# One PSUM pool, copied-out values, additions in thirds and one ranking tile per half in a fused attention and routed feed-forward kernel

## The chip, the cores and the metric

The kernel runs on one core of a Trainium2 chip. The metric is the device time of one execution in microseconds (us); of three runs before the change the median is 877.36 us (875.94 to 880.07). All times below are us unless ns is written. Engines: PE is TensorE (PEld its weight loads), DVE is VectorE, ACT is ScalarE, POOL is GpSimd, SP is SyncE, which issues most of the DMAs.

## The reference, cut to what matters

```
B, H, S, D = 8, 8, 1152, 64;  Sp = 576;  Dm = 512;  F = 1024;  capacity = 128
q_pool = q.reshape(B, H, Sp, 2, D).mean(axis=3)
attn   = softmax(q_pool @ k.T / sqrt(D))              # 576 x 1152 for each head
x      = attn @ v                                     # joined over heads: (B, 576, 512)
for b in range(B):
    scores  = x[b] @ w_gate
    top     = the 128 rows of largest score
    out[b]  = x[b]
    out[b, top] += sigmoid(scores[top]) * (relu(x[b, top] @ w1) @ w2)
```

All is float32.

## The kernel before

**Pairs and halves.** The class `_Plain` does the work (a second path, `_any_scores`, is entered only if the softmax sums leave a safe range). Two heads are a pair: the eight images `b` have four pairs each, and a pair is done in two halves of 288 pooled query rows, so there are 64 halves, 8 in each image. `run()` writes the order out by hand, and each engine executes its own list in that order. One turn `h` of its loop does `scores(h)`, `folded(h)`, then `weighted(h-1)`, `drained(h-1)` and `between(...)`. On PE this gives the score matmuls of one half, the value matmuls of the half before it, then whatever `between` adds.

**Scores (L724 to L740).** Nine tiles, each of two banks of PSUM for the two heads. PE fills a tile (`sc<-qT,kT`), ACT takes the exponent into `p`. The pool `ps_sc` has three such tiles, so the matmuls of the fourth wait for the exponents of the first, and so on.

**Sums (`folded`, L755 to L781).** POOL adds the tiles 0 to 2 to the tiles 3 to 5 of `p` in one instruction (`acc`, 128x1728), DVE folds the tiles 6 to 8 (`fold<-p`) and `acc` (`fold<-acc`), and makes `sum`.

**Values (`weighted`, L742 to L753; `drained`, L783 to L791).** 36 matmuls accumulate `av` in the one tile of the pool `ps_av`; DVE transposes it from PSUM into `avb`.

**A finished pair (`normalized`, L793 to L834).** After each second half PE makes the row sums (`ps<-sum,merge`, L796) in the one tile of the pool `ps_ms`, DVE copies them (`sums`) and inverts them (`rec`), POOL makes `x` and then `prod` (L828), DVE reduces that to `part` (L834). Behind it DVE's list goes on with what `between` adds, then with the transposes `kT` and `qT` of the next pair (`prepare_pair`, every second half), whose `qp` POOL adds after `prod`. The score matmuls of the next pair need `qT`.

**Routing (`routed`, L844 to L1033).** It is a generator, started when an image's last pair is finished. `between`, called once in each half, sends each generator in `self.routing` one piece further. The pieces before the change are, in the eight halves after the start:

1. L870: the score row, spread by PE, copied by ACT to `sc_row`.
2. L656: five small transposes into the tile `ps` (the one of L796), copied by DVE to `gate_sc`; the gate's exponent on ACT (L887); ranking tiles 0 and 1 on DVE. A ranking tile is two comparisons `cmp` and a `tie`, which reads `sc_row` and `before` from SBUF.
3. Ranking tiles 2 and 3.
4. Ranking tile 4, `meta`, and the selection matrices `pick`.
5. L953: ten small matmuls make the list `index` and `own_gate`; POOL gathers the chosen rows `xe` by DMA (L965).
6. L980: `xe` transposed by PE, copied by ACT to `xeT`.
7. L992: first feed-forward layer, 64 matmuls in one two-bank tile, with two ACT instructions (L1000).
8. L1007: second layer, 16 matmuls; DVE adds it to `xe` (L1014), POOL scatters it (L1022).

After the loop `ending` is set and the rest of the routing runs without pauses between ranking tiles.

Of the kernel before, what the change touches and what calls it, by code (L numbers as in the profile page):

```python
# [10 lines left out]
P = 128  # L11
BLK = 32

G = 3
F32 = mybir.dt.float32
# [519 lines left out]
class _Plain:  # L535
# [10 lines left out]
    def __init__(self, ctx, tc, q, k, v, moe_w_gate, moe_w1, moe_w2, capacity, out):  # L546
# [54 lines left out]
    def constants(self):  # L601
# [29 lines left out]
        self.columns(self.token, line_f, self.misc())  # L631
# [92 lines left out]
    def scores(self, half):  # L724
# [4 lines left out]
        for c in range(self.NC):  # L729
            sc = self.ps_sc.tile([P, 2, 512], F32, name="sc")  # L730
# [11 lines left out]
    def weighted(self, half):  # L742

        nc, n = self.nc, self.HALF
        half["av"] = self.ps_av.tile([P, 512], F32, name="av")
        for c in range(self.NC):
            for j in range(2):
                nc.tensor.matmul(  # L748
                    half["av"][j * self.D : (j + 1) * self.D, 0:n],
# [4 lines left out]
                )  # L754

    def folded(self, half):
# [3 lines left out]
        acc = self.work.tile([P, G * 2 * self.HALF], F32, name="acc")  # L760
        groups = p.rearrange("p g u j n -> p g (u j n)")
# [4 lines left out]
        for a, of in enumerate((groups[:, 2, :], acc[:, :])):  # L766
            nc.vector.tensor_reduce(  # L767
                fold[:, a, :],
                of.rearrange("p (m d) -> p m d", d=BLK),
                AX.X,  # L770
                ALU.add,
                apply_transpose=True,
            )
# [9 lines left out]
    def drained(self, half):  # L783
        pair, n, hb = half["pair"], self.HALF, self.HB
        if half["s"] == 0:
# [3 lines left out]
            half["av"][:, 0:n],  # L789
# [48 lines left out]
    def misc(self):  # L838
        return self.ps_ms.tile([P, 512], F32, name="ps")

    def wide(self):
        return self.ps_sc.tile([P, 2, 512], F32, name="sc")

    def routed(self, b, xs, part):  # L844
# [23 lines left out]
        ps = self.wide()  # L868
# [18 lines left out]
        nc.scalar.activation(gate[:, :], gate[:, :], AF.Exp, scale=-1.0)  # L887
# [4 lines left out]
        for t, rows in tiles:  # L892
# [32 lines left out]
            if t % 2 == 1 and not self.ending:  # L925
                yield
        nc.vector.tensor_scalar(
# [11 lines left out]
        for s0, w in self.slots:  # L939

            pick = ffn.tile([P, NT, P], F32, name="pick")
            for t, rows in tiles:
# [6 lines left out]
                )  # L949
            at_ps = yield  # L950
# [27 lines left out]
            pv = self.wide()[:, 0, :].rearrange("p (c n) -> p c n", n=P)  # L978
# [8 lines left out]
            for f0 in range(0, self.NFC, 8):  # L987
                pv = self.wide().rearrange("p b (c n) -> p (b c) n", n=P)
                nf = min(8, self.NFC - f0)
                for f in range(nf):  # L990
# [8 lines left out]
                    if f % 4 == 3:  # L999
                        nc.scalar.activation(  # L1000
# [181 lines left out]
```

## Time and profile before

| | us |
|---|---|
| three runs, median | 877.36 |
| three runs, range | 875.94 to 880.07 |
| profiled execution, its own time | 876.72 |
| profiled execution, span of its instructions | 874.90 |
| PE busy in the span | 786.5 |
| DVE busy | 504.4 |
| POOL busy | 396.1 |
| ACT busy | 345.0 |

The span is what the trace shows; 1.82 us of the profiled execution lie around it. The views read are the busy table of the page, the busy time by stretch, the chain of waits and the timelines of single engines. In a timeline row the first two numbers are the start, in us from the span's start, and the duration; the bracket is the idle time of the engine just before, and what ended it.

### The profile page before, as it was taken

The numbers are of one execution on the slowest core, as the hardware profiler recorded it, in microseconds if no ns is written. First come the engines' busy times: TensorE is split into PE (matmuls) and PEld (weight loads), VectorE is DVE, ScalarE is ACT, GpSimd is POOL, SyncE is SP. The second block draws the span as 40 slices with busy tenths as digits, with TensorE's granted clock in tenths as the row PEclk, the third lists the DMA queues.
The fourth block names the chain that finished last, engine by engine and source line by source line (L and its number), as shares of the span: only waits on it lengthen the run. The fifth ranks groups of instructions, "written<-read, shape, count | busy, mean of one in ns | idle before, by whom it ended". The sixth has DMA issues, their size and how long they took to land.

```text
span 874.9 us, 13669 instructions
## 1 busy us (share of the span) xinstructions
PE 786.5 (90%) x5503; PEld 478.2 (55%) x5503; DVE 504.4 (58%) x848; ACT 345.0 (39%) x617; POOL 396.1 (45%) x188
## 2 busy tenths in 40 slices
PE   6979979899798998899988999889979899799936
PEld 4545545565455654565555655556545565456634
DVE  3556666735677347762667535774556836576250
ACT  5435445342444243442443334443345342445000
POOL 3546645444555254552444535453535445554110
PEclk9999999999999998999998999899999999999968
DMA  9997786674767578395764928849286773761020
GB/s 135 255 144 106 102 146 92 98 96 101 98 72 115 75 132 97 51 129 63 148 95 54 121 42 148 96 76 124 56 123 88 102 96 93 102 77 26 14 79 16
DMA packets 453545, 84.95 MB, mean 97 GB/s; under 512 B 450656, under 2 KB 450656, under 8 KB 453216
## 3 DMA queue, kind: packets, MB, share of 16 engines
q1 hardware_dynamic: 447456, 79.20, 62.6%
q0 software_dynamic: 1280, 4.20, 1.7%
q10 hardware_dynamic: 4736, 0.59, 0.7%
q8 instruction: 45, 0.74, 0.4%
q14 instruction: 28, 0.23, 0.1%
HBM read 72.42 MB, written 20.97 MB: 107 GB/s over the span
## 4 chain that ended last, share of the span: by engine, by line
PE 58%; DVE 14%; POOL 11%; ACT 7%; DMA 4%; issue 3%; SPq 2%; ACTq 0%; POOLq 0%; DVEq 0%
PE sc L733 24%; PE av L748 20%; PE sc L992 7%; POOL acc L762 7%; ACT p L740 6%; PE sc L1007 6%; DVE fold L767 3%; DVE tie L916 3%; POOL prod L828 2%; DMA qb<-in_q_dram 2%; POOL x L815 2%; DMA xe<-xs,index 2%; DVE part L834 1%; DVE kT L715 1%; SPq L685 1%
## 5 line engine op out<-in xcount | busy, mean ns | idle before, releaser
L740 ACT ACTIVATE p<-sc 128x576 f32<-128x576 f32 x576 | 323.3, 683 | 253.5 <-issue 193.4
L733 PE MATMUL sc<-qT,kT 64*128 64x288 f32 x2304 | 340.6, 448 | 40.8 <-ACT p L740 20.6
L762 POOL TENSOR_TENSOR acc<-p 128x1728 f32<-128x1728 f32 x64 | 247.3, 3865 | 209.2 <-ACT p L740 208.2
L748 PE MATMUL av<-p,v_sb 128*64 128x288 f32 x2304 | 293.5, 409 | 0.7 <-DVE avb L787 0.7
L733 PEld LDWEIGHTS sc<-qT,kT 64*128 64x128 f32 x2304 | 201.4, 196 | 166.1 <-ACT p L740 110.2
L748 PEld LDWEIGHTS av<-p,v_sb 128*64 128x64 f32 x2304 | 159.8, 137 | 127.0 <-issue 22.2
L767 DVE TRANSPOSE_TENSOR_REDUCE fold<-p 128x54 f32<-128x1728 f32 x64 | 125.8, 1965 | 167.2 <-ACT p L740 167.2
L767 DVE TRANSPOSE_TENSOR_REDUCE fold<-acc 128x54 f32<-128x1728 f32 x64 | 126.1, 1971 | 27.2 <-POOL acc L762 27.2
L815 POOL TENSOR_TENSOR x<-avb,rec 128x576 f32<-128x576 f32 x32 | 37.0, 1157 | 120.7 <-DVE rec L814 120.7
L834 DVE TENSOR_REDUCE part<-prod 128x18 f32<-128x576 f32 x32 | 24.1, 753 | 88.0 <-POOL prod L828 88.0
L992 PE MATMUL sc<-xeT,w 128*128 128x128 f32 x512 | 64.1, 286 | 6.2 <-ACT hT L1000 5.5
L992 PEld LDWEIGHTS sc<-xeT,w 128*128 128x128 f32 x512 | 61.1, 199 | 11.2 <-ACT hT L1000 7.0
L1007 PE MATMUL sc<-w,hT 128*128 128x512 f32 x128 | 56.8, 597 | 0.0
L712 POOL TENSOR_TENSOR qp<-qb 128x576 f32<-128x576 f32 (+1 forms) x33 | 45.1, 1368 | 21.1 <-DMA qb<-in_q_dram 21.0
L715 DVE STREAM_TRANSPOSE kT<-kb 128x1152 f32<-128x1152 f32 (+1 forms) x33 | 44.0, 1333 | 14.1 <-DMA kb<-in_k_dram 14.1
L828 POOL TENSOR_TENSOR prod<-x,w_gate 128x576 f32<-128x576 f32 x32 | 44.9, 1404 | 2.5
L1000 ACT ACTIVATE hT<-sc 128x512 f32<-128x512 f32 x16 | 9.6, 597 | 90.6 <-PE sc L992 90.6
L965 POOL DMA_INDIRECT xe<-xs,index x8 | 8.5, 1067 | 70.3 <-DVE own_gate L963 58.9
L1007 PEld LDWEIGHTS sc<-w,hT 128*128 128x128 f32 x128 | 23.7, 190 | 26.8 <-issue 26.8
L787 DVE STREAM_TRANSPOSE avb<-av 128x288 f32<-128x288 f32 x64 | 30.4, 476 | 11.9 <-PE av L748 11.3
L916 DVE SCALAR_TENSOR_TENSOR tie<-sc_row,gate_sc,before 128x128 f32<-128x128 f32 (+1 forms) x40 | 37.1, 928 | 0.0
L1022 POOL DMA_INDIRECT out_dram<-xe,index x8 | 12.2, 1530 | 50.0 <-DVE line L855 26.8
(64 smaller groups left out, 246.4 us busy)
## 6 DMA issues: line engine op xcount, KB each, us to landing
v_sb<-in_v_dram SPq DMA_DIRECT2D x64, 288.0 KB, 5.3
kb<-in_k_dram SPq DMA_DIRECT2D x124, 144.0 KB, 4.6
qb<-in_q_dram SPq DMA_DIRECT2D x124, 144.0 KB, 4.8
xs<-x SPq DMA_DIRECT2D x128, 72.0 KB, 2.3
out_dram<-xs SPq DMA_DIRECT2D x8, 1152.0 KB, 6.0
w<-in_moe_w_dram SPq DMA_DIRECT2D x2, 2048.0 KB, 11.0
kb<-in_k_dram SPq DMA_DIRECT2D x8, 72.0 KB, 4.1
qb<-in_q_dram ACTq DMA_DIRECT2D x8, 72.0 KB, 4.3
```

The source lines that it names most:

```text
L712: nc.gpsimd.tensor_tensor(out=qp[:, qs, :], in0=pair["q"][:, qs, 0, :], in1=pair["q"][:, qs, 1, :], op=ALU.add)
L715: nc.vector.transpose(pair["kT"][:, i * nk * BLK : (i + 1) * nk * BLK], pair["k"][:, ks, :].rearrange("p n d -> p (n d)"),)
L733: nc.tensor.matmul(sc[:, j, 0:n], lhsT=pair["kT"][rows, c * P : (c + 1) * P], rhs=pair["qT"][rows, qs], start=True, stop=True,)
L740: nc.scalar.activation(p[:, c // G, c % G, :, :], sc[:, :, 0:n], AF.Exp, scale=self.scale)
L748: nc.tensor.matmul(half["av"][j * self.D : (j + 1) * self.D, 0:n], lhsT=half["pair"]["v"][:, j, c, :], rhs=half["p"][:, c // G, c % G, j, ...
L762: nc.gpsimd.tensor_tensor(out=acc[:, :], in0=groups[:, 0, :], in1=groups[:, 1, :], op=ALU.add)
L767: nc.vector.tensor_reduce(fold[:, a, :], of.rearrange("p (m d) -> p m d", d=BLK), AX.X, ALU.add, apply_transpose=True,)
L815: nc.gpsimd.tensor_tensor(out=x[:, hp, :, :], in0=pair["avb"][:, :, :], in1=rec[:, :].unsqueeze(2).broadcast_to([P, self.QB, BLK]), op=ALU ...
L828: nc.gpsimd.tensor_tensor(out=prod[:, :, :], in0=x[:, hp, :, :], in1=self.w_gate[:, hp : hp + 1, :].broadcast_to([P, self.QB, BLK]), op=AL ...
L916: nc.vector.scalar_tensor_tensor(out=tie[0:rows, 0:rows], in0=sc_row[0:rows, at : at + rows], scalar=own, in1=self.before[0:rows, 0:rows], ...
L992: nc.tensor.matmul(pv[:, f, 0:w], lhsT=self.w1[:, c, (f0 + f) * P : (f0 + f + 1) * P], rhs=xeT[:, c, 0:w], start=(c == 0), stop=(c == self ...
L1007: nc.tensor.matmul(ps[0:w, 0 : self.Dm], lhsT=hT[:, f, 0:w], rhs=self.w2[:, f, :], start=(f == 0), stop=(f == self.NFC - 1),)
```

## The change

The pools `ps_sc`, `ps_av` and `ps_ms` become one pool `psum` of four tiles of two banks (`banks()`). Everything that is in PSUM takes its tile there in turn: nine score tiles of a half, the values, the tile of the row sums, and the routing's. The values are copied by ACT to SBUF (`av`, L754 after) at the end of `weighted`, and DVE transposes that copy. POOL's addition becomes three of 128x576, each of which needs two tiles of `p`. The gate's exponent moves behind the last ranking tile. Each ranking tile is followed by a pause, and one more pause is put after `pick`, so that the routing of one image now takes eleven halves: it is still at work in the first three halves of the image after next, where two generators are in the list, the newer served first. The first feed-forward layer uses one bank of each of two tiles.

```diff
-        self.ps_sc = pool("ps_sc", 3, space=psum)
-        self.ps_av = pool("ps_av", 1, space=psum)
-        self.ps_ms = pool("ps_ms", 1, space=psum)
+        self.psum = pool("psum", 4, space=psum)
...
         for c in range(self.NC):
-            sc = self.ps_sc.tile([P, 2, 512], F32, name="sc")
+            sc = self.banks()
...
     def weighted(self, half):
-        half["av"] = self.ps_av.tile([P, 512], F32, name="av")
+        av = self.banks()[:, 0, :]
...
+        half["av"] = self.small.tile([P, n], F32, name="av", bufs=2)
+        nc.scalar.copy(half["av"][:, :], av[:, 0:n])
...
-        nc.gpsimd.tensor_tensor(
-            out=acc[:, :], in0=groups[:, 0, :], in1=groups[:, 1, :], op=ALU.add
-        )
+        for u in range(G):
+            nc.gpsimd.tensor_tensor(
+                out=acc[:, u, :], in0=units[:, 0, u, :], in1=units[:, 1, u, :], op=ALU.add
+            )
...
-    def misc(self):
-        return self.ps_ms.tile([P, 512], F32, name="ps")
-
-    def wide(self):
-        return self.ps_sc.tile([P, 2, 512], F32, name="sc")
+    def banks(self):
+        return self.psum.tile([P, 2, 512], F32, name="ps")
...
-        nc.scalar.activation(gate[:, :], gate[:, :], AF.Exp, scale=-1.0)
...
-            if t % 2 == 1 and not self.ending:
+            if t < NF and not self.ending:
                 yield
+        nc.scalar.activation(gate[:, :], gate[:, :], AF.Exp, scale=-1.0)
...
+            if not self.ending:
+                yield
             at_ps = yield
...
-            for f0 in range(0, self.NFC, 8):
-                pv = self.wide().rearrange("p b (c n) -> p (b c) n", n=P)
-                nf = min(8, self.NFC - f0)
-                for f in range(nf):
+            for f0 in range(0, self.NFC, 4):
+                pv = self.banks()[:, 0, :].rearrange("p (c n) -> p c n", n=P)
+                for f in range(4):
...
-                    if f % 4 == 3:
-                        nc.scalar.activation(
-                            hT[:, f0 + f - 3 : f0 + f + 1, 0:w], pv[:, f - 3 : f + 1, 0:w], AF.Relu
-                        )
+                nc.scalar.activation(hT[:, f0 : f0 + 4, 0:w], pv[:, :, 0:w], AF.Relu)
...
     def between(self, pair):
-        ps = self.misc()
+        ps = self.banks()[:, 0, :]
...
-        for unit in list(self.routing):
+        for unit in self.routing[::-1]:
```

The first place is PE's list in the second half of one image and the first of the next. `ps<-meta,pick` is L953, `ps<-ident,xe` the transposes of the gathered rows, `xeT,w` and `w,hT` the two feed-forward layers. Before:

```order
L748 MATMUL av<-p,v_sb 64x288 x18
L796 MATMUL ps<-sum,merge 128x36
L980 MATMUL sc<-ident,xe 128x128 x4
L733 MATMUL sc<-qT,kT 128x288 x18
L748 MATMUL av<-p,v_sb 64x288 x18
L992 MATMUL sc<-xeT,w_115 128x128 x32
L733 MATMUL sc<-qT,kT 128x288 x18
L748 MATMUL av<-p,v_sb 64x288 x18
L796 MATMUL ps<-sum,merge 128x36
L1007 MATMUL sc<-w_116,hT 128x512 x8
```

The same two and the next three halves after the change, where the row sums of the pair, L953 and then the next image's first routing pieces stand between:

```order
L797 MATMUL ps<-sum,merge 128x36
L953 MATMUL ps<-meta,pick 128x3 x5
L731 MATMUL ps<-qT,kT 128x288 x18
L746 MATMUL ps<-p,v_sb 64x288 x18
L868 MATMUL ps<-diag,ones 128x288 x2
L980 MATMUL ps<-ident,xe 128x128 x4
L731 MATMUL ps<-qT,kT 128x288 x18
L746 MATMUL ps<-p,v_sb 64x288 x18
L797 MATMUL ps<-sum,merge 128x36
L654 MATMUL ps<-ident,sc_row 128x1 x4
L654 MATMUL ps<-ident,sc_row 64x1
L991 MATMUL ps<-xeT,w_109 128x128 x32
```

The feed-forward of an image has moved from its sixth to eighth half of routing to the ninth to eleventh, and L953 from the fifth to the eighth.

The second place is the end of PE's list. Before, from the last half's values on:

```order
L748 MATMUL av<-p,v_sb 64x288 x18
L796 MATMUL ps<-sum,merge 128x36
L1007 MATMUL sc<-w_116,hT 128x512 x8
L870 MATMUL sc<-diag,ones 128x288 x2
L656 MATMUL ps<-ident,sc_row 128x1 x4
L656 MATMUL ps<-ident,sc_row 64x1
L953 MATMUL ps<-meta,pick 128x3 x5
L1049 MATMUL ps<-low,ones 1x2
L980 MATMUL sc<-ident,xe 128x128 x4
L992 MATMUL sc<-xeT,w_115 128x128 x32
L1007 MATMUL sc<-w_116,hT 128x512 x8
```

After it, from the row sums of the last pair on:

```order
L953 MATMUL ps<-meta,pick 128x3 x5
L868 MATMUL ps<-diag,ones 128x288 x2
L980 MATMUL ps<-ident,xe 128x128 x4
L654 MATMUL ps<-ident,sc_row 128x1 x4
L654 MATMUL ps<-ident,sc_row 64x1
L991 MATMUL ps<-xeT,w_109 128x128 x32
L953 MATMUL ps<-meta,pick 128x3 x5
L1045 MATMUL ps<-low,ones 1x2
L1003 MATMUL ps<-w_110,hT 128x512 x8
L980 MATMUL ps<-ident,xe 128x128 x4
L991 MATMUL ps<-xeT,w_109 128x128 x32
L1003 MATMUL ps<-w_110,hT 128x512 x8
```

The whole feed-forward of the seventh image now stands among the pieces of the eighth image's routing, its first layer behind L654 and its second behind L953.

The third place is ACT's list around the exponents (`p`) of the first routed image. Before:

```order
L877 COPY sc_row<-sc 128x576
L740 ACTIVATE p<-sc 128x576 x9
L887 ACTIVATE gate<-gate 128x5
L740 ACTIVATE p<-sc 128x576 x36
```

After:

```order
L875 COPY sc_row<-ps 128x576
L738 ACTIVATE p<-ps 128x576 x9
L754 COPY av<-ps 128x288
L738 ACTIVATE p<-ps 128x576 x9
L754 COPY av<-ps 128x288
L738 ACTIVATE p<-ps 128x576 x9
L754 COPY av<-ps 128x288
L738 ACTIVATE p<-ps 128x576 x9
L754 COPY av<-ps 128x288
L738 ACTIVATE p<-ps 128x576 x9
L754 COPY av<-ps 128x288
L924 ACTIVATE gate<-gate 128x5
```

A copy of the values stands between the exponents of every two halves, and the gate's exponent four halves later.

## Rows read from the trace of the kernel before

**Rows 1.** Stretches of the span: length, busy time by engine, PE clock, DMA share, GB/s.

```profile
51.04:100.78 49.74, 49.74 (x367) 29.14 (x367) 33.21 (x34) 25.19 (x45) 29.92 (x12) 0.97 0.92 123
100.78:206.36 105.58, 98.22 (x688) 59.54 (x687) 64.38 (x110) 43.10 (x77) 50.68 (x23) 0.97 0.65 96
206.36:732.14 525.78, 487.70 (x3436) 294.92 (x3435) 314.35 (x520) 214.60 (x385) 245.84 (x110) 0.97 0.66 96
732.14:819.46 87.32, 79.95 (x598) 50.27 (x598) 55.16 (x94) 37.27 (x67) 41.41 (x18) 0.98 0.46 71
819.46:874.90 55.44, 34.48 (x160) 22.71 (x159) 13.67 (x61) 3.22 (x6) 6.20 (x5) 0.80 0.14 43
```

**Rows 2.** The same view for the eight steps of one image, columns as above.

```profile
310.68:321.32 10.64, 10.64 (x77) 6.02 (x77) 8.15 (x9) 5.00 (x9) 6.88 (x3) 1.00 0.54 160
321.32:332.92 11.60, 10.26 (x81) 6.03 (x80) 5.46 (x8) 5.63 (x10) 3.91 (x2) 1.00 1.18 132
332.92:346.91 13.99, 11.35 (x74) 6.79 (x73) 8.72 (x20) 5.40 (x10) 7.71 (x4) 0.76 0.60 79
346.91:356.76 9.85, 9.85 (x77) 5.68 (x75) 7.29 (x17) 5.00 (x9) 3.86 (x1) 1.00 0.93 99
356.76:369.94 13.18, 10.90 (x83) 6.66 (x83) 10.31 (x26) 5.00 (x9) 7.73 (x4) 1.00 0.14 23
369.94:381.05 11.11, 10.43 (x78) 6.21 (x78) 7.83 (x8) 5.00 (x9) 4.92 (x2) 1.00 1.05 153
381.05:398.82 17.77, 17.08 (x138) 12.68 (x137) 9.22 (x13) 6.18 (x11) 7.75 (x4) 1.00 0.95 115
398.82:415.58 16.76, 16.76 (x92) 8.57 (x91) 5.94 (x8) 5.59 (x10) 6.42 (x3) 1.00 0.26 41
```

**Rows 3.** Chain of waits in that image: start, us, what.

```profile
310.75 4.96 PE sc L733 x36
315.71 4.52 PE av L748 x36
```

**Rows 4.** Timelines of ACT and PEld in the second step.

```profile
321.43 0.64 ACT L877 COPY sc_row<-sc 128x576 f32<-128x576 f32 x1 [4.90 <-PE sc L870]
322.17 4.99 ACT L740 ACTIVATE p<-sc 128x576 f32<-128x576 f32 x9
...
322.87 0.30 PEld L733 LDWEIGHTS sc<-qT,kT 64*128 64x128 f32 x4 [0.28 <-ACT p L740]
323.42 0.30 PEld L733 LDWEIGHTS sc<-qT,kT 64*128 64x128 f32 x4 [0.24 <-ACT p L740]
```

**Rows 5.** Timeline of PE in that image.

```profile
332.55 0.44 PE L656 MATMUL ps<-ident,sc_row 1*128 1x1 f32 x5 [1.34 <-DVE sums L806]
...
337.71 4.76 PE L733 MATMUL sc<-qT,kT 64*128 64x288 f32 x24 [2.64 <-ACT p L740]
...
369.94 5.01 PE L733 MATMUL sc<-qT,kT 64*128 64x288 f32 x36 [1.45 <-DVE qT L719]
...
395.05 3.84 PE L992 MATMUL sc<-xeT,w 128*128 128x128 f32 x32 [0.69 <-ACT hT L1000]
```

**Rows 6.** Timelines of ACT and DVE, second and third step.

```profile
336.91 0.21 ACT L887 ACTIVATE gate<-gate 128x5 f32<-128x5 f32 x1 [9.74 <-DVE rank_parts L890]
...
332.17 0.32 DVE L806 TENSOR_SCALAR sums<-ps 64x18 f32<-64x18 f32 x2
...
335.54 0.75 DVE L834 TENSOR_REDUCE part<-prod 128x18 f32<-128x576 f32 x1 [2.75 <-POOL prod L828]
```

**Rows 7.** Timelines of DVE and POOL in the fifth step.

```profile
362.70 3.69 DVE L916 SCALAR_TENSOR_TENSOR tie<-sc_row,gate_sc,before 64x64 f32<-64x64 f32 x1
...
362.47 3.83 POOL L762 TENSOR_TENSOR acc<-p 128x1728 f32<-128x1728 f32 x1
```

**Rows 8.** Timeline of PE after the last half.

```profile
842.58 2.35 PE L953 MATMUL ps<-meta,pick 128*128 128x3 f32 x10 [7.03 <-DVE pick L943]
...
850.58 6.56 PE L992 MATMUL sc<-xeT,w 128*128 128x128 f32 x32 [0.68 <-ACT xeT L983]
```

More of the change, by code (lines that the diff above doesn't have):

```diff
@@ L630, in constants @@
         self.token = const.tile([P, self.NT], F32, name="token")
-        self.columns(self.token, line_f, self.misc())
+        self.columns(self.token, line_f, self.banks()[:, 0, :])
         self.same = const.tile([P, BLK], F32, name="same")
@@ L748, in weighted @@
                 nc.tensor.matmul(
-                    half["av"][j * self.D : (j + 1) * self.D, 0:n],
+                    av[j * self.D : (j + 1) * self.D, 0:n],
                     lhsT=half["pair"]["v"][:, j, c, :],
@@ L754, in weighted @@
                 )
+        half["av"] = self.small.tile([P, n], F32, name="av", bufs=2)
+        nc.scalar.copy(half["av"][:, :], av[:, 0:n])
     def folded(self, half):
         nc, nb, p, pair = self.nc, 2 * self.HB, half["p"], half["pair"]
-        acc = self.work.tile([P, G * 2 * self.HALF], F32, name="acc")
-        groups = p.rearrange("p g u j n -> p g (u j n)")
-        nc.gpsimd.tensor_tensor(
-            out=acc[:, :], in0=groups[:, 0, :], in1=groups[:, 1, :], op=ALU.add
-        )
+        acc = self.work.tile([P, G, 2 * self.HALF], F32, name="acc")
+        units = p.rearrange("p g u j n -> p g u (j n)")
+        for u in range(G):
+            nc.gpsimd.tensor_tensor(
+                out=acc[:, u, :], in0=units[:, 0, u, :], in1=units[:, 1, u, :], op=ALU.add
+            )
         fold = self.small.tile([P, 2, G * nb], F32, name="fold")
-        for a, of in enumerate((groups[:, 2, :], acc[:, :])):
+        for a, of in enumerate((units[:, 2, :, :], acc[:, :, :])):
             nc.vector.tensor_reduce(
                 fold[:, a, :],
-                of.rearrange("p (m d) -> p m d", d=BLK),
+                of.rearrange("p u (m d) -> p (u m) d", d=BLK),
                 AX.X,
@@ L788, in drained @@
             pair["avb"].rearrange("p n d -> p (n d)")[:, half["s"] * n : (half["s"] + 1) * n],
-            half["av"][:, 0:n],
+            half["av"][:, :],
         )
@@ L867, in routed @@
         flat = diag.rearrange("p n i -> p (n i)")
-        ps = self.wide()
+        ps = self.banks()
         for s in range(2):
@@ L986, in routed @@
             hT = ffn.tile([P, self.NFC, P], F32, name="hT")
-            for f0 in range(0, self.NFC, 8):
-                pv = self.wide().rearrange("p b (c n) -> p (b c) n", n=P)
-                nf = min(8, self.NFC - f0)
-                for f in range(nf):
+            for f0 in range(0, self.NFC, 4):
+                pv = self.banks()[:, 0, :].rearrange("p (c n) -> p c n", n=P)
+                for f in range(4):
                     for c in range(self.ND):
@@ L1047, in outside @@
             )
-        ps = self.misc()
+        ps = self.banks()[:, 0, :]
         nc.tensor.matmul(ps[0:1, 0:2], lhsT=self.ones[:, 0:1], rhs=low[:, :], start=True, stop=True)
@@ L1065, in between @@
     def between(self, pair):
-        ps = self.misc()
+        ps = self.banks()[:, 0, :]
         if pair:
             self.normalized(pair, ps)
-        for unit in list(self.routing):
+        for unit in self.routing[::-1]:
             try:
```

2 lines of the change are left out of this document (removed).

## Prediction

> **What bounds the kernel now.** I read the busy time by stretch first. PE is at work in nearly the whole of the span between 51 and 819 us: 487.70 of 525.78 in the five middle images, with DVE at 314.35 and DMAs at 96 GB/s [rows 1]. So what counts is PE's list: the work in it and the places where it stops. One image in eight steps (from the first score matmul of one half to that of the next) shows both [rows 2]. The chain of waits gives the bare step: scores 4.96, values 4.52, together 9.48 [rows 3]. The fourth step, 9.85, is that and the row sums, 0.37. The first has L870 besides, 1.16; the eighth has 0.37 and the second layer, 6.91; the seventh the first layer, 8.29. The rest is waiting: in the second step L656 waits 1.34 for `sums` [rows 5]. In the third, 13.99 long, PE stands 2.64 for ACT, whose exponents stand behind the gate's exponent; that waited for DVE, which had waited for `prod` [rows 5, 6]. PE's clock was 0.76 of full in that step, so part of it ran at 1.2 GHz, the lower of its two levels, instead of 2.4, after that stop [rows 2]. In the fifth, 13.18, the list of chosen rows (1.37) and the next pair's `qT` come late, because DVE's `tie` took 3.69 beside POOL's `acc` [rows 7].
>
> Two more stops are small and everywhere. From the fourth tile on the score matmuls follow ACT, one tile freed at a time [rows 4]: nine tiles take 4.96 where the values, with as many matmuls over as many columns, take 4.52 [rows 3]. And in the seventh step the first layer's second half waits 0.69 for its first [rows 5].
>
> **The change, part by part.**
>
> *Four tiles for the scores.* With four the fifth tile waits for the first exponent. ACT begins 0.85 into the step and frees one tile in about 0.55 (nine in 4.99) [rows 4]; PE without a wait needs 4.52/9 = 0.50. The first exponent ends about 1.5 into the step, the fifth tile is due at 2.0, the ninth at 4.0 and its place is free at 3.7. So the wait goes: 0.4 a step, between nothing and the 0.44 that separates the two phases. A bare step becomes 9.08.
>
> *Copies on ACT.* 128x288 has no row; 128x576 from PSUM took 0.64 [rows 4]. I take 0.4, between 0.3 and 0.64. The copy comes when the values end, while ACT waits for the next first score tile, which needs 0.85, so ACT hides it. Not hidden is that DVE gets `avb` some 0.6 later, and `sums` stands behind it: about 11.0 after the step's start, where now it is 11.2 (332.17 and 0.32, less 321.32) [rows 6]. PE meanwhile comes 0.4 earlier, so where it waits for `sums` it waits longer.
>
> *One pool.* The row sums' tile is handed on to the scores. In a step after a finished pair the fourth score tile takes it: due at 1.5, free at about 1.6, so 0.15. In the first step the tile holds `index` and `own_gate` too, which stand behind `part` in DVE's list; `part` ends 4.1 after `sums` began [rows 6]. That is 0.6 on the fifth score tile. What is queued behind these waits on PE are the values; ACT waits with them.
>
> *Additions in thirds.* 3.83/3 = 1.28 each [rows 7]. The first can begin two exponents earlier, but `fold<-acc` stands behind `fold<-p` on DVE, so the sums gain 0.3 at most, counted above. The gain is that `tie` can get in after one third instead of a whole addition.
>
> *Gate's exponent.* Four halves later its input is long there. The third step loses its stop, the lower clock behind it, all above the bare step: 13.99 to 9.08 plus what is added there.
>
> *Ranking and routing slower.* The fourth step now holds two ranking tiles and has no wait in its 9.85, with DVE busy for 7.29 [rows 2]; one tile a step fits, but for what its `tie` may wait. The feed-forward goes to the first three steps of the next image, where L654 and DVE's late work lie beside it.
>
> The eight steps after, in the new order:
>
> 1. 9.08 + L868 1.16 + L980 0.6 + the wait for `own_gate` 0.6 = 11.45. The gather has a step and lands in 6 or so.
> 2. L654 behind `sums` ends at 11.5 as now; the first layer 8.29 less its 0.69: 19.1.
> 3. 9.08 + 6.91 = 16.0.
> 4. 9.08 + 0.37 = 9.45.
> 5. 9.08 + 0.15 + 0.5 for a `qT` that a `tie` of up to one third delays = 9.75.
> 6. 9.45.
> 7. Ranking tile 4 and `pick`. Now this is the fifth step, 13.18, of which the tie gives back 3.69 - 1.28 - 0.3 = 2.1, to 11.1; DVE comes 0.8 late from tile 3 a step earlier: 11.9.
> 8. 9.08 + 0.37 + L953 1.37 + its wait for `sums`, now 1.34 plus the 0.4 = 1.7: 12.5.
>
> The sum is 99.6, where the same image has 104.90: 5.3 an image.
>
> **The sum.** Against the profiled execution, 876.72:
> - up to 51.04: nothing; DMAs set it. 51.04 to 100.78: four steps of 0.4, **1.6**.
> - The first routed image, 105.58 [rows 1], has no feed-forward any more: 99.6 less 0.6, 0.6, 7.6 and 6.9, plus 1.6 in the third step (nothing covers the wait for `gate_sc`, some 4.2 behind `sums`) and 1.6 for DVE's lateness behind it: 87.1, **18.5** less.
> - Five images: **26.5** less.
> - The last stretch, 87.32, against steps 1 to 7, without a next pair's `qT` in the seventh (9.95): 85.1, **2.2** less.
> - The end, 55.44. The last L953 comes some 1.4 sooner, since `line` no longer waits behind the seventh image's second layer; the seventh image's first layer fills the time before the last L953 (now 18 us after the values). Its second layer then stands before the last L980 and costs about 4 beyond the gather. A warmer PE gives 1.0 at L953 (2.35 for 1.37) and 2.7 at L992 (6.56 for 3.84) [rows 8]. Together **0**, between 4 less and 4 more.
>
> 48.8 in all: 827.9. The median lies 0.64 above the profiled execution, so 828.6; I say 829.
>
> **The rivals.**
>
> *A tie is blocked by all three thirds.* It starts and then ends with POOL's addition [rows 7]; no row shows what happens when another addition follows at once. If the next third goes first, ties in steps 5, 6 and 7 wait 2.6, 1 and 2.6 longer: 6 an image, times 6.6 images is 41: 870. The Trainium skill (SBUF — State Buffer, "Who interferes with whom") says that a VectorE instruction with two SBUF inputs is blocked until the GpSimd instruction that began first is finished; by that the tie gets in after one third, which is the forecast, and the trace agrees for one addition (3.69 beside 3.83). For the rival speaks only that POOL's list is full there.
>
> *The scores stay at ACT's pace.* If a fourth tile doesn't help, because one place is always held by values or row sums, the 0.4 of 62 steps is gone: 25, so 854. Against it: the values' tile is free 0.6 after the step's start, well before it is due.
>
> *DVE holds the scores: slower.* The row sums' tile ties PE to DVE's list, in which `sums` stands behind ranking, folds and ties. If in the steps after ranking tiles 2 and 4, and in the eighth, `sums` comes later by the tie's 3.4 (3.69 less 0.3) and each such stop drops the clock as in the third step now (24 matmuls in 4.76, where 24/36 of 4.52 is 3.0, so 1.7) [rows 3, 5], that is 5.1 in three steps of 6.6 images: 101, so 930. It decides for slower from 49/20 = 2.5 in each of these 20 steps. For it: one tile after another is handed from DVE to PE. Against it: DVE has 63 of 105 us busy in an image [rows 2], and stops of 1.45 left the clock at 1.00. The Trainium skill (TensorE: Matmul & The Clock Gate, "A second HAM failure mode: psum-queue depth-cycling") speaks for this case: a kernel that cycles through PSUM banks stops PE briefly between groups so often that its clock swings between its levels. The row of the third step shows such a swing after 2.64; no row shows it for stops under 1.5.
>
> *Fewer waits than counted.* If DVE keeps up and no step waits beyond what PE does, steps 5, 7, 8 and 1 lose 0.65, 2.8, 1.0 and 0.6: 5 an image, 33: 796.
>
> **How the numbers follow.** Forecast 0.60 (its own range, from the bounds of 0.4 per step, the copies and the end, 812 to 846); blocked ties 0.12; ACT's pace 0.12; fewer waits 0.06; slower by DVE 0.10. The range reaches to the blocked ties on the one side and half way to the fewer waits on the other: 808 to 871. A measurement here tells 0.5%, 4.4 us, from no change. Faster by more: all but the last rival and a part of the blocked ties, 0.87; the same 0.04; slower 0.09.
>
> **What would show it.** Score phases of 4.5 to 4.6; the third step without an ACT stop; ties no longer than about 1.6; `sums` some 11.0 after the step's start; in the steps without feed-forward 9.1 and 9.5; the seventh image's first layer inside the gap before the last L953; images of about 100 us. The forecast is wrong if score tiles often wait for DVE, if PE's clock in the middle falls below 0.95, or if the end grows by more than 4.

## The result, and the profile of the changed kernel

The changed kernel takes 844.5 us (median; 841.5 to 844.7) where the kernel before took 878.6 on the same chip: a ratio of 0.961, 95% interval 0.957 to 0.964, or 34 us less. The forecast was 829, its range 808 to 871. The direction and the range hold; of the 48.8 us that were summed, some 34 came. In two of the kernels below one execution was over 1.5% slower than the fastest of the same kernel; it is left out of their medians.

The profiled execution took 844.71, with a span of 843.0. The stretches of its span that answer to [rows 1], in the same columns (the first row again covers the four steps before the first ranking, the last one the end):

```profile
52.27:101.86 49.59, 49.59 (x366) 32.98 (x367) 32.86 (x34) 27.34 (x50) 31.58 (x24) 0.94 0.84 121
101.86:190.25 88.39, 80.35 (x604) 53.30 (x605) 64.88 (x107) 44.76 (x83) 50.13 (x37) 0.96 0.72 108
190.25:702.10 511.85, 477.86 (x3438) 320.37 (x3439) 319.55 (x520) 231.65 (x425) 254.72 (x191) 0.97 0.65 98
702.10:785.82 83.72, 81.87 (x606) 54.57 (x608) 50.31 (x88) 39.96 (x74) 44.59 (x34) 1.00 0.43 78
785.82:843.00 57.18, 42.76 (x239) 30.58 (x235) 19.23 (x72) 5.20 (x10) 6.62 (x6) 0.88 0.16 46
```

Against the forecast of each stretch, the start comes 1.2 late (52.27 for 51.04; it lies between 49.9 and 52.7 in the traces of these kernels, and no cause was sought), the first stretch is 1.4 too long (49.59 for 49.74 - 1.6), the first routed image 1.3 (88.39 for 87.1), the five images 12.6 (511.85 for 525.78 - 26.5), the last stretch 1.4 too short (83.72 for 85.1), the end 1.7 too long (57.18 for 55.44). That is 16.8, the whole miss of the profiled execution (844.7 for 827.9). Three quarters of it lie in the five middle images. The eight steps of one of them, as in [rows 2]:

```profile
292.40:304.06 11.66, 11.12 (x83) 7.07 (x83) 7.97 (x9) 5.83 (x11) 8.28 (x7) 1.00 0.72 177
304.06:322.54 18.48, 17.20 (x144) 13.76 (x143) 10.13 (x21) 6.79 (x13) 8.06 (x6) 1.00 0.67 97
322.54:338.69 16.15, 16.15 (x90) 8.87 (x89) 5.66 (x10) 5.99 (x11) 4.14 (x3) 1.00 0.92 111
338.69:348.27 9.58, 9.58 (x76) 6.01 (x75) 4.45 (x3) 5.22 (x10) 5.18 (x4) 1.00 0.07 27
348.27:357.41 9.14, 9.14 (x73) 5.92 (x73) 6.30 (x16) 5.17 (x10) 7.55 (x6) 1.00 0.21 34
357.41:366.83 9.42, 9.42 (x76) 6.67 (x74) 9.38 (x12) 5.61 (x11) 4.74 (x4) 1.00 1.27 136
366.83:380.27 13.44, 9.43 (x74) 6.16 (x73) 10.54 (x26) 5.75 (x12) 8.01 (x6) 0.96 0.39 60
380.27:394.85 14.58, 13.50 (x85) 9.49 (x86) 9.46 (x11) 5.93 (x10) 4.96 (x4) 0.80 0.90 121
```

The forecast was 11.45, 19.1, 16.0, 9.45, 9.75, 9.45, 11.9 and 12.5. Six steps are within 0.7 of it, and together 0.8 below it. The seventh is 1.5 too long, the eighth 2.1. In the seventh PE is busy for 9.43 of 13.44 us: it stops. In the eighth PE is busy nearly throughout, but with a granted clock of 0.80. PE's timeline shows both (start, duration, what, and in brackets the idle time before it and what ended that), the first row from an undisturbed step:

```profile
322.54 4.64 PE L731 MATMUL ps<-qT,kT 64*128 64x288 f32 x36
...
380.27 7.50 PE L731 MATMUL ps<-qT,kT 64*128 64x288 f32 x36 [3.98 <-DVE qT L717]
...
393.70 1.25 PE L953 MATMUL ps<-meta,pick 128*128 128x3 f32 x9 [1.08 <-DVE sums L807]
```

The 36 score matmuls take 7.50 here and 4.64 in the undisturbed step, so part of them ran at 1.2 instead of 2.4 GHz after the stop. And `qT` is late because of what stands ahead of it in DVE's list. DVE and POOL in the seventh step:

```profile
373.03 1.24 DVE L913 SCALAR_TENSOR_TENSOR tie<-sc_row,gate_sc,before 64x64 f32<-64x64 f32 x1
374.21 1.37 DVE L925 TENSOR_SCALAR gate<-gate 128x5 f32<-128x5 f32 x1
375.50 0.15 DVE L930 COPY meta<-token 128x5 f32<-128x5 f32 x1
375.57 1.37 DVE L931 TENSOR_SCALAR meta<-token 128x5 f32<-128x5 f32 x1
377.11 1.06 DVE L941 TENSOR_SCALAR pick<-slot_f,rank 128x128 f32<-128x128 f32 x5
...
379.39 0.73 DVE L717 STREAM_TRANSPOSE qT<-qp 128x576 f32<-128x576 f32 x1
...
372.79 4.12 POOL L763 TENSOR_TENSOR acc<-p 128x576 f32<-128x576 f32 x3
```

The tie gets in after the first third, as forecast (against 3.69 in [rows 7]). But then an operation on 128x5 numbers takes 1.37 and so does a second one; in the end of the same trace, where POOL adds nothing, they take 0.16 and 0.15. Each ends when a third ends. 1.24 + 1.37 + 1.37 = 3.98 is what the tie alone with the same two behind it took before (3.69 and twice some 0.16). The thirds gave DVE nothing in this step.

### The profile page after: what moved, and what is told of

Read it like the earlier page. It is cut to its first block, busy times and chain, and to the rows that moved or that the text cites. A ratio compares the mean times of both kernels' runs of the same rounds, so it can differ in the third digit from the quotient of the medians.

```text
span 843.0 us, 13988 instructions
## 1 busy us (share of the span) xinstructions
PE 767.9 (91%) x5503; PEld 515.8 (61%) x5503; DVE 510.1 (61%) x848; ACT 371.8 (44%) x681; POOL 410.6 (49%) x316
## 4 chain that ended last, share of the span: by engine, by line
PE 55%; DVE 21%; ACT 7%; POOL 7%; DMA 3%; SPq 3%; issue 2%; ACTq 0%; POOLq 0%; DVEq 0%
PE ps L731 22%; PE ps L746 17%; DVE fold L768 9%; PE ps L991 7%; ACT p L738 7%; PE ps L1003 7%; POOL prod L829 3%; DMA qb<-in_q_dram 2%; POOL x L816 2%; DVE tie L913 2%; POOL acc L763 1%; SPq L689 1%; SPq L683 1%; DVE kT L713 1%; DVE gate L925 1%
## 5 line engine op out<-in xcount | busy, mean ns | idle before, releaser
L738 ACT ACTIVATE p<-ps 128x576 f32<-128x576 f32 x576 | 325.3, 678 | 137.9 <-PE ps L731 87.8
L731 PE MATMUL ps<-qT,kT 64*128 64x288 f32 x2304 | 326.2, 434 | 41.3 <-DVE qT L717 36.9
L763 POOL TENSOR_TENSOR acc<-p 128x576 f32<-128x576 f32 x192 | 266.2, 1415 | 162.9 <-ACT p L738 162.8
L731 PEld LDWEIGHTS ps<-qT,kT 64*128 64x128 f32 x2304 | 240.8, 199 | 114.5 <-issue 47.3
L746 PE MATMUL ps<-p,v_sb 128*64 128x288 f32 x2304 | 293.3, 409 | 0.0
L746 PEld LDWEIGHTS ps<-p,v_sb 128*64 128x64 f32 x2304 | 159.9, 137 | 125.6 <-ACT p L738 21.2
L754 ACT COPY av<-ps 128x288 f32<-128x288 f32 x64 | 25.5, 398 | 222.4 <-PE ps L746 218.5
L991 PE MATMUL ps<-xeT,w 128*128 128x128 f32 x512 | 61.4, 282 | 0.8 <-ACT xeT L983 0.7
L991 PEld LDWEIGHTS ps<-xeT,w 128*128 128x128 f32 x512 | 59.9, 197 | 1.2 <-ACT xeT L983 1.1
L1003 PE MATMUL ps<-w,hT 128*128 128x512 f32 x128 | 57.0, 598 | 0.0
```

The source lines that it names most:

```text
L731: nc.tensor.matmul(sc[:, j, 0:n], lhsT=pair["kT"][rows, c * P : (c + 1) * P], rhs=pair["qT"][rows, qs], start=True, stop=True,)
L738: nc.scalar.activation(p[:, c // G, c % G, :, :], sc[:, :, 0:n], AF.Exp, scale=self.scale)
L746: nc.tensor.matmul(av[j * self.D : (j + 1) * self.D, 0:n], lhsT=half["pair"]["v"][:, j, c, :], rhs=half["p"][:, c // G, c % G, j, :], star ...
L763: nc.gpsimd.tensor_tensor(out=acc[:, u, :], in0=units[:, 0, u, :], in1=units[:, 1, u, :], op=ALU.add)
L991: nc.tensor.matmul(pv[:, f, 0:w], lhsT=self.w1[:, c, (f0 + f) * P : (f0 + f + 1) * P], rhs=xeT[:, c, 0:w], start=(c == 0), stop=(c == self ...
L1003: nc.tensor.matmul(ps[0:w, 0 : self.Dm], lhsT=hT[:, f, 0:w], rhs=self.w2[:, f, :], start=(f == 0), stop=(f == self.NFC - 1),)
```

## The experiments

Twelve kernels were run, each compared with the kernel before on its own chip, where that has a median of 877.8 to 879.0. Times are medians; differences between two of the kernels are taken between their medians.

| kernel | us | ratio to before, 95% |
|---|---|---|
| the change | 844.5 | 0.957 to 0.964 |
| the change with one whole addition | 892.1 | 1.012 to 1.018 |
| the change, gate's exponent back | 845.4 | 0.960 to 0.965 |
| the change, old pauses | 849.8 | 0.960 to 0.971 |
| the change, old PSUM pools | 849.1 | 0.962 to 0.969 |
| before, gate's exponent moved | 887.2 | 1.007 to 1.015 |
| before, thirds | 879.5 | 0.998 to 1.004 |
| the change, `pick` and `meta` a turn later | 842.6 | 0.954 to 0.963 |
| the change, accumulator outputs | 846.0 | 0.958 to 0.966 |
| the change, `part` behind the routing | 840.1 | 0.955 to 0.963 |
| both of these | 808.7 | 0.919 to 0.926 |
| both, old PSUM pools | 821.7 | 0.932 to 0.942 |
| both, own tile for the routing | 791.9 | 0.899 to 0.904 |

### Undoing one part at a time

**One whole addition** (`whole_add`).

```diff
-        for u in range(G):
-            nc.gpsimd.tensor_tensor(
-                out=acc[:, u, :], in0=units[:, 0, u, :], in1=units[:, 1, u, :], op=ALU.add
-            )
+        nc.gpsimd.tensor_tensor(
+            out=acc.rearrange("p u n -> p (u n)"),
+            in0=units[:, 0, :, :].rearrange("p u n -> p (u n)"),
+            in1=units[:, 1, :, :].rearrange("p u n -> p (u n)"),
+            op=ALU.add,
+        )
```

> The changed kernel with GpSimd's three additions per half made one again (128x1728). Theory: in the seventh step of an image three DVE instructions (the tie and two small TENSOR_SCALARs, 1.24, 1.37 and 1.37 us) wait for one third each, as the tie alone waited 3.69 for the whole addition before, so the thirds give nothing there: the time stays at 844.5, within 4 us, and with one tie of about 3.7 us the two TENSOR_SCALARs take 0.2 us each. Rival (the sum of the prediction): a tie that waits for one third alone is worth 2.1 us in the seventh step of 6.6 images, so the whole addition costs 14 us: 858.

Both expectations for the whole time fell: 892, slower than the kernel before. For the seventh step the theory held to the hundredth. The fifth to eighth step of an image:

```profile
364.06:376.11 12.05, 9.43 (x73) 6.16 (x73) 9.21 (x16) 5.62 (x11) 7.74 (x4) 1.00 0.16 26
376.11:387.22 11.11, 11.11 (x74) 7.91 (x75) 8.91 (x12) 5.65 (x10) 3.87 (x1) 0.85 1.26 150
387.22:400.65 13.43, 9.42 (x73) 6.15 (x73) 10.53 (x26) 5.74 (x12) 7.73 (x4) 1.00 0.19 31
400.65:414.90 14.25, 12.61 (x86) 9.35 (x87) 9.58 (x11) 5.72 (x10) 4.96 (x2) 0.87 1.08 124
```

DVE's timeline in the seventh:

```profile
393.41 3.69 DVE L915 SCALAR_TENSOR_TENSOR tie<-sc_row,gate_sc,before 64x64 f32<-64x64 f32 x1
...
397.03 0.16 DVE L927 TENSOR_SCALAR gate<-gate 128x5 f32<-128x5 f32 x1
```

The seventh step is 13.43 here and 13.44 with thirds: one long wait of the tie, or three short ones. What the thirds are worth lies in the steps with one tie and nothing small behind it: the fifth falls from 12.05 to 9.14, the sixth, whose clock is 0.85 after the stop in the fifth, from 11.11 to 9.42. The prediction had these two right (9.75 and 9.45), but its sum names the thirds as a gain only in the seventh step. Two more steps of the traced image are longer at a lower clock, the first (12.13 at 0.88, for 11.66) and the second (20.49 at 0.92, for 18.48).

**The gate's exponent back** (`gate_back`).

```diff
             out=gate[:, :], in0=sc[:, :], scalar1=-88.0, scalar2=None, op0=ALU.max
         )
+        nc.scalar.activation(gate[:, :], gate[:, :], AF.Exp, scale=-1.0)
...
-        nc.scalar.activation(gate[:, :], gate[:, :], AF.Exp, scale=-1.0)
```

> The changed kernel with the gate's exponent in its old place in ACT's list, ahead of the ranking. Rival (the prediction): the third step stands 2.64 us for ACT and then runs at the lower clock again, 4.5 us an image, 30 us in all: 874. Theory: in the new order the second step holds the feed-forward's first layer, and DVE's input of the exponent (319.1 in the traced image) is there before the third step's exponents start (322.5); only the Relus behind the exponent come 1 to 1.5 us late: 844 to 854.

845.4: the theory. In the old place the exponent still waits on ACT for DVE, but with time to spare where the second step holds a feed-forward. ACT's timeline in the second step:

```profile
318.67 0.21 ACT L885 ACTIVATE gate<-gate 128x5 f32<-128x5 f32 x1 [5.56 <-DVE rank_parts L888]
...
322.87 1.74 ACT L738 ACTIVATE p<-ps 128x576 f32<-128x576 f32 x3 [0.18 <-PE ps L731]
```

It is done four us before the third step's exponents start, since the second step now holds the first layer, 7.41 us of PE. So the third step lost its stop ([rows 5], 2.64) to the new place of the feed-forward. The move of the exponent, to which the prediction gave it, is worth nothing there. Where there is no feed-forward, in the first routed image, PE does stop longer with the exponent in its old place, 2.06 for 1.38.

**The old pauses** (`pauses_back`).

```diff
-            if t < NF and not self.ending:
+            if t % 2 == 1 and not self.ending:
                 yield
...
-            if not self.ending:
-                yield
             at_ps = yield
```

> The changed kernel with the old pauses of the routing: two ranking tiles per half and no empty turn behind pick, so that the feed-forward stands in the seventh and eighth step of the same image. Theory: the first routed image gets its feed-forward back (15 us) and the seventh image's leaves the end, where it stood in gaps; in the other images the tie of tile 4 and the two small TENSOR_SCALARs move to the fifth step, where they cost the same as now in the seventh: 856 to 862. Rival: the slower routing itself costs the two late steps (13.44 and 14.58 us) their 5 us an image, so the old pauses are faster by some 10 us: 834.

849.8, which is neither. The first routed image, the five middle images and the end, from the last half's values on as in the tables above:

```profile
99.80:200.46 100.66, 94.19 (x688) 62.43 (x687) 65.98 (x110) 46.28 (x86) 53.17 (x39) 0.98 0.68 100
200.46:710.38 509.92, 481.73 (x3436) 316.70 (x3435) 318.19 (x520) 233.00 (x425) 257.64 (x190) 0.95 0.68 99
...
794.39:848.70 54.31, 33.81 (x160) 22.26 (x159) 13.78 (x61) 3.62 (x7) 6.21 (x5) 0.80 0.14 44
```

The slower routing leaves the middle images about as long as they were (102.0 in the mean with the old pauses, 102.4 without). It saves 12.3 us in the first routed image (100.66 to 88.39) and pays 2.9 back at the end (54.31 to 57.18); 2.1 more go before the first routed image and 1.9 in the five images, and 0.3 come back in the last stretch. That is 5.7 by the traces and 5.3 by the medians, hardly clear of the noise: the executions with the old pauses lie at 843.1 to 852.2. The rival of this experiment, that the slower routing costs the two late steps their time, is out.

**The old pools** (`old_pools`, and `repaired_old_pools` on a kernel that comes below).

```diff
-        self.psum = pool("psum", 4, space=psum)
+        self.ps_sc = pool("ps_sc", 3, space=psum)
+        self.ps_av = pool("ps_av", 1, space=psum)
+        self.ps_ms = pool("ps_ms", 1, space=psum)
...
```

> The changed kernel with the old three PSUM pools (three score tiles, one for the values, one for the row sums), all else as changed. Theory: the score phases go back from 4.64 to the 4.96 of before, 0.32 us in 62 steps, 20 us: 864, with the images' other waits unchanged. Rival: ACT's pace is hidden by the stops that are left, and the shared tiles' waits on DVE (0.54 us in the first step) go away: 844 to 850.

849.1, inside the rival's range, although the score phases did grow, by 0.39 where nothing disturbs them (PE's timeline; 4.64 with four tiles):

```profile
352.10 5.03 PE L733 MATMUL sc<-qT,kT 64*128 64x288 f32 x36
...
384.44 5.02 PE L733 MATMUL sc<-qT,kT 64*128 64x288 f32 x36 [3.51 <-DVE qT L719]
```

The fourth tile is worth what was forecast (0.4) in a bare step, and by the medians 4.6 us in the whole time, hardly clear of the noise: the five executions lie at 846.4 to 855.3, and the profiled one is the slowest, 10.6 above that of the changed kernel. Where the gain goes is seen in part in the traced image. Its third to sixth step are 0.3 to 0.7 longer than in the changed kernel, the seventh is 0.4 shorter, and the eighth takes 12.17 at a clock of 1.00 for 14.58 at 0.80: behind a stop of 3.51 the score matmuls kept their pace there (second row), and the lower clock came a step later (12.51 at 0.86). In the next image they took 7.35 behind the same stop. The rest is seen by taking the late `qT` away first.

> The kernel with the accumulator outputs and part behind the routing (808.7), with the old three PSUM pools. Undone in the changed kernel, the fourth score tile cost only 4.6 us, though each score phase grew by 0.39. Theory: there the longer phases lay in time in which PE waited for qT anyway; where that wait is gone, 0.39 in 62 steps shows in full, 24 us: 828 to 835. Rival: the tile of the row sums, no longer shared, gives back as much as the fourth tile is worth: 809 to 815.

821.7 against 808.7: 13.0, between the two. By the traces of these two an image is 98.73 and 95.43, and the profiled executions are 821.15 and 801.82, 19.3 apart; the other executions of the faster kernel lie at 808.6 to 812.7 and are not profiled. Theory and rival each hold in part: 62 phases of 0.39 are 24, and PE's waits for `sums`, whose tile is no longer shared, fall from 18.7 to 14.0, which leaves about the 19.3 of the traces. The theory's reason, that the longer phases lay in the wait for `qT`, fits one step of eight; in the traced image above the clock gave back more.

### One part alone on the kernel before

**The exponent** (`before_gate`) and **the thirds** (`before_thirds`), with the same edits as above, applied to the kernel before.

> The kernel before with the gate's exponent moved behind the ranking and nothing else. Theory (the prediction's third step): PE's stop of 2.64 us and the lower clock behind it go, 13.99 to about 9.5 in 7 images, 31 us: 847. Rival: the stop only moves, to the next thing that comes late (qT in the fifth step, or the list's matmuls, which now wait for the exponent): 865 to 878.

887.2: slower by 1.1%, above both expectations. The stop on ACT went and PE waited for DVE instead. PE's list of waits (for what, us in total, times, longest):

```profile
PE ps L953 <- DVE pick L943: 32.8, 8, 7.0
PE sc L733 <- DVE qT L719: 27.5, 17, 6.2
```

In the kernel before the same two are 12.8 and 20.2, with 20.6 for ACT. The third step falls from 13.99 to 11.54, the fifth grows from 13.18 to 16.19. That DVE's list has no room behind the third step is how I read this; no run moved DVE's work alone there.

> The kernel before with GpSimd's additions in thirds and nothing else. Theory: in the fifth step of an image the tie, the two small TENSOR_SCALARs and pick stand one behind the other beside these additions; with thirds each waits for one, and DVE loses the same 3.7 us: 874 to 880. Rival (the prediction's term): the tie gives back 2.1 us, in 6.6 images 14 us: 864.

879.5, no difference: the theory. DVE in the fifth step shows the same row of three as the changed kernel:

```profile
360.69 1.24 DVE L919 SCALAR_TENSOR_TENSOR tie<-sc_row,gate_sc,before 64x64 f32<-64x64 f32 x1
...
361.86 1.37 DVE L930 TENSOR_SCALAR gate<-gate 128x5 f32<-128x5 f32 x1
...
363.22 1.37 DVE L936 TENSOR_SCALAR meta<-token 128x5 f32<-128x5 f32 x1
```

### Taking the late qT away

**`pick` and `meta` a turn later** (`meta_pick_late`): DVE's small operations and `pick` stand behind the empty turn.

```diff
+            if not self.ending:
+                yield
             pick = ffn.tile([P, NT, P], F32, name="pick")
...
-            if not self.ending:
-                yield
+            nc.vector.tensor_scalar(
+                out=gate[:, :], in0=gate[:, :], scalar1=1.0, scalar2=None, op0=ALU.add
+            )
+            meta = ffn.tile([P, NT, 3], F32, name="meta")
...
             at_ps = yield
```

> The changed kernel with the two small TENSOR_SCALARs (gate, meta), their copy and reciprocal, and the five of pick one turn later, behind the empty turn. Theory: DVE loses only the tie (about 1.3 us) to the additions in the seventh step, qT ends some 3.7 us earlier, PE no longer stops 3.98 us for it, the clock stays at 1.00 in the eighth step: the two steps take about 9.6 and 12.2 instead of 13.44 and 14.58, 5.4 us an image in 6.6 images, 36 in all: 808. Rival: qT is late for another reason (POOL's qp behind prod), and the two steps keep their time: 844.

842.6. The seventh step did fall, to 9.85, with a stop of 0.38. But the time came back one step later. DVE and PE in the eighth:

```profile
379.20 3.56 DVE L933 TENSOR_SCALAR pick<-slot_f,rank 128x128 f32<-128x128 f32 x5
...
387.99 2.17 PE L953 MATMUL ps<-meta,pick 128*128 128x3 f32 x9 [3.55 <-DVE sums L807]
```

There the five of `pick` meet the next additions (3.56 for 1.06), `sums` behind them comes later, L953 waits 3.55 for 1.08 and runs at the lower clock. The mechanism was right and the place only moved: here too the plain operations that stand beside the additions lose the time of them.

**Accumulator outputs** (`accum`): the two small operations and `pick` get a spare accumulator output.

```diff
                     op0=ALU.is_equal,
+                    op1=ALU.add,
+                    accum_out=spare[0:rows, :],
...
```

> The changed kernel with a spare accumulator output on the two small TENSOR_SCALARs (gate, meta) and on the five of pick, which makes them the same form as the comparisons (cmp); nothing is moved. Theory: that form doesn't wait for GpSimd's additions (a cmp of 64x64 took 0.27 us beside one): gate and meta take 0.2 instead of 1.37 each, pick some 1.7 instead of 1.06, qT comes 1.6 us earlier, the seventh step falls from 13.43 to about 11.8, and the eighth keeps part of its lower clock: 10 to 18 us less in all, 826 to 834. Rival (every DVE instruction beside GpSimd's additions waits, whatever its form): 844.

846.0, as the rival had it, but not by the rival's reason. DVE in the seventh step:

```profile
373.92 0.14 DVE L926 TENSOR_SCALAR_CACHE_REDUCE gate<-gate 128x5 f32<-128x5 f32 x1
...
374.00 1.30 DVE L932 COPY meta<-token 128x5 f32<-128x5 f32 x1
375.21 0.15 DVE L933 TENSOR_SCALAR_CACHE_REDUCE meta<-token 128x5 f32<-128x5 f32 x1
...
375.54 0.35 DVE L944 TENSOR_SCALAR_CACHE_REDUCE pick<-slot_f,rank 128x128 f32<-128x128 f32 x1
```

In this form the two take 0.14 and 0.15 beside the additions. The copy between them, which I had left as it was, now meets the second third and takes 1.30 for 0.15, and five of `pick` with their reads of the accumulator take 1.9 for 1.06. The step falls to 13.00 only. The Trainium skill (SBUF — State Buffer, "Who interferes with whom") says that copy, cast and tensor_scalar, but not tensor_scalar in the form that also writes its accumulator, can take the ports that VectorE shares with GpSimd. The rows agree for the copy (1.30), the plain form (1.37) and the form with the accumulator (0.14); no cast stands beside an addition here. An edit that takes the copy off as well was not tried.

**`part` behind the routing** (`part_late`), so that the ranking lies in the time in which DVE waits for POOL's `prod` (2.75, [rows 6]).

```diff
-        nc.vector.tensor_reduce(pair["part"][:, hp, :], prod[:, :, :], AX.X, ALU.add)
+        pair["prod"] = prod
...
             except StopIteration:
                 self.routing.remove(unit)
+        if pair:
+            self.nc.vector.tensor_reduce(
+                pair["part"][:, pair["hp"], :], pair["prod"][:, :, :], AX.X, ALU.add
+            )
```

> The changed kernel with DVE's sum of prod into part behind the routing, and without the accumulator outputs. Theory (each GpSimd operation on two SBUF inputs holds up one plain DVE operation): the ranking starts 3.5 us earlier in the seventh step, but tie, gate, meta and three of pick each wait for one of GpSimd's x, prod, qp and the three thirds, up to 377 in the traced image, so qT is no earlier than about 379 to 380; only own_gate's 0.54 in the first step goes: 836 to 844. Rival (the order alone was what the last kernel gained by): the same as with the accumulators, 808.

840.1: the theory, with an interval that overlaps the changed kernel's. `pick`, now beside `qp` and the thirds, takes five times its time, and the seventh step is 12.97:

```profile
366.33 5.53 DVE L941 TENSOR_SCALAR pick<-slot_f,rank 128x128 f32<-128x128 f32 x5
```

**Both** (`part_accum`).

> The same accumulator outputs, and DVE's sum of prod into part behind the routing instead of ahead of it, so that ranking lies in the 2.75 us in which DVE waits for GpSimd's prod. Theory: the ranking of the seventh step ends some 3 to 4 us earlier, qT some 4.8 us earlier than the 380.1 of the traced image, which is ahead of PE's need; steps seven and eight take about 9.9 and 12.2 instead of 13.44 and 14.58, and own_gate no longer holds the first step for 0.54: 6.5 us an image in 6.6 images, 43 in all: 802. Rival: what is won there is lost at the next wait (sums ahead of the list's matmuls, or the end), as when pick was moved: 835 to 845.

808.7, near the theory's 802. Each edit alone gave -1.5 and 4.4 us, the two together 35.8. The seventh and eighth step of an image:

```profile
348.05:357.45 9.40, 9.29 (x74) 6.16 (x73) 9.11 (x33) 5.35 (x12) 7.50 (x6) 1.00 0.35 55
357.45:369.58 12.13, 10.71 (x85) 7.87 (x87) 9.47 (x11) 5.73 (x11) 5.58 (x5) 1.00 1.23 146
```

Without the stop the clock stays at 1.00. This is the forecast of the two steps (11.9 and 12.5) and more. It shows what kept `qT` late in the changed kernel: DVE's wait for `prod` ahead of the ranking and the waits of its plain operations for POOL behind it. With the accumulator outputs alone PE's stop was still 3.54, with the reorder alone 3.69; with both it is gone, and the lower clock behind it too.

**An own tile** (`part_accum_own`). L654 and the list (L953, here L958) take a PSUM tile of their own in place of columns in the tile of the row sums.

```diff
-            at_ps = yield
-            ps = at_ps[:, 72:75]
+            yield
+            ps = self.banks()[:, 0, 0:3]
...
```

> The kernel with the accumulator outputs and part behind the routing, and besides a PSUM tile of its own for the transposes of the scores (L654) and for the list (L958), which shared the tile of the row sums and so waited 1.3 to 1.4 us for DVE's sums, seven times each (18.7 us in all). Theory: both waits go, 16 to 18 us: 791 to 794. Rival: one more tile a turn goes through the four places, DVE holds it, and the scores stop for it as long as PE waited before: 808.

791.9: the theory, and the best of all, 9.8% below the kernel before. One wait in PE's list is new (0.3 in the kernel with both edits):

```profile
PE ps L868 <- DVE diag L857: 10.4, 6, 1.9
```

## Why the prediction was right, and where it wasn't

**What held.** PE's list sets the time, and six of eight steps came out within 0.7 us by the forecast's sums. Score phases are 4.64 where 4.5 to 4.6 was said, bare steps 9.14 where it was 9.08. ACT's copy is 0.40, as taken. The wait for `own_gate` is 0.54 for 0.6. The longest tie is 1.33 (1.6 was the bound), so the rival in which a tie waits for all three thirds is out. The scores did not stay at ACT's pace, and the mean clock of the middle is 0.97, so the slower rival, in which DVE's hold on the score tiles drops the clock in three steps, is out as well. The longest wait of this kind is 1.38, in the third step of the first routed image, where the sum had 1.6.

**What failed** is the seventh step, in the words "of which the tie gives back 3.69 - 1.28 - 0.3 = 2.1". The tie gave it back, and the next two operations of DVE took it. The prediction looked at one instruction where POOL's list acts on all that stand beside it: as long as three thirds run, three operations wait. What follows the tie in DVE's list in the kernel before (gate, copy, meta, `pick`) was not priced. The runs with a whole addition (13.43 for 13.44) and with thirds alone (879.5) show that the term is nothing.

**Its consequence** is the eighth step. The forecast had a wait for `sums` there and no clock; PE's stop for `qT` grew to 3.98 and the next stretch ran at 0.80, 7.50 for 4.64. The stop is one piece now because L953 no longer stands in it. PE in the kernel before, in the fifth step of the image of [rows 2] and behind that of the next image:

```profile
367.13 1.36 PE L953 MATMUL ps<-meta,pick 128*128 128x3 f32 x10 [0.83 <-DVE pick L943]
...
475.00 7.55 PE L733 MATMUL sc<-qT,kT 64*128 64x288 f32 x36 [1.45 <-DVE qT L719]
```

The prediction took the clock's drop from the row of 2.64, but only in the rival on DVE's tiles; yet by its own sum the seventh step held a stop of 2.8 (11.9 less 9.08), longer than that one, and no clock was priced behind it. And its "stops of 1.45 left the clock at 1.00" was read from one image: behind the same stop the score matmuls took 6.3 to 7.6 in four of the seven images that have it in that trace, as in the second row. With the stop gone the clock is 1.00 (12.13 for 14.58). These two steps make 1.5 + 2.1 = 3.6 an image; the others give 0.8 back.

**Right for the wrong reason.** The third step's stop is gone, and not by the move of the gate's exponent: undone, the move costs 0.9 us, within the noise; alone on the kernel before it makes the time 9 longer. The feed-forward in the second step covers it.

**Mis-sized terms.** The end was to stay (0) and grew by 1.7. The last L953 was to come 1.4 sooner behind the last half's values than the 18.5 of before; it came 20.5 behind them. `pick` was done at 809.07, but the seventh image's first layer, which stands ahead of L953 in PE's list and takes 7.41 elsewhere, took 9.50. The rows:

```profile
801.53 9.50 PE L991 MATMUL ps<-xeT,w 128*128 128x128 f32 x64
...
808.01 1.06 DVE L941 TENSOR_SCALAR pick<-slot_f,rank 128x128 f32<-128x128 f32 x5
...
810.87 1.26 PE L953 MATMUL ps<-meta,pick 128*128 128x3 f32 x10
```

The first stretch lost 1.4 of its 1.6, at a clock of 0.94 for 0.97; nothing was tried on that. ACT's copies were not undone by themselves.

**The parts don't add.** Undone one at a time they cost 47.6 (thirds), 5.3 (pauses), 4.6 (pools) and 0.9 (exponent), the last three with intervals that overlap the change's own; the change gave 34.1. The thirds are worth 47.6 in the changed kernel and nothing in the kernel before. That this hangs on one ranking tile a step in place of two is how I read it; no run has whole additions with the old pauses in the changed kernel.

## What to carry over

When a long operation on one engine blocks another engine's work, cutting it into pieces freed that work in these runs only where a single blocked instruction stood there; list all that follow it, with their forms, and count one wait for each piece. Price a step by undoing it in the new order, not only by its row in the old one: a stop can vanish because other work now lies in front of it, and a gain can lie inside a wait that is still there. Two edits that each give nothing can be worth 36 us together, when either wait alone is enough to make the same input late. Read a row in every image before it stands for all: the clock behind one and the same stop was not the same in each.

## What the hardware did that I had not expected

- An operation's size says little about what it costs beside GpSimd: 128x5 numbers took 1.37 instead of 0.16 us as TENSOR_SCALAR, 1.30 instead of 0.15 as COPY, and 0.14 as TENSOR_SCALAR with an accumulator output.
- One DVE operation was not let in between GpSimd's. In the kernel with both edits `diag`, a TENSOR_TENSOR on two SBUF inputs, took 6.22 us, where it takes 0.79 in the changed kernel:

```profile
372.45 6.22 DVE L857 TENSOR_TENSOR diag<-line,same 128x576 f32<-128x576 f32 x1
...
371.48 1.06 POOL L970 DMA_INDIRECT xe<-xs,index  x1 [0.15 <-issue]
372.56 1.41 POOL L710 TENSOR_TENSOR qp<-qb 128x576 f32<-128x576 f32 x1
373.93 4.12 POOL L763 TENSOR_TENSOR acc<-p 128x576 f32<-128x576 f32 x3
```

  It begins 0.11 before `qp` and ends after all four of GpSimd's operations, while ties and plain operations got in after one. The Trainium skill (SBUF — State Buffer, "Who interferes with whom") says that whichever instruction is issued first gets the shared ports for its whole length; by that `diag` would have waited for one operation at most, and the row differs. Whether the gather's descriptors, which GpSimd was writing as `diag` began, are the reason was not tried. It is the 10.4 us of L868 that is left in the fastest kernel.
- After PE's stops of 3.98 and 3.69 us (the changed kernel, and the one with `part` behind the routing) the granted clock of the next step was 0.80 and 0.88; after one of 0.38 the score matmuls that follow take 4.63, as in the steps at 1.00. But the length of a stop doesn't tell the clock behind it: with the old PSUM pools the score matmuls took 5.02 in one image and 7.35 in the next, both behind 3.51 or 3.50, and in the kernel before 5.01 to 7.55 behind 1.45.
